# Attention and a two-layer network in one kernel: the words ahead of chunk 2 in another order

## The chip, the cores and the metric

The kernel runs on one core of one Trainium2 chip. The metric is device time in microseconds, and lower is better. A core has five engines with a queue each: TensorE (PE in the profile, its weight loads PEld), VectorE (DVE), ScalarE (ACT), GpSimd (POOL) and SyncE (SP). They run beside each other and wait for each other on semaphores. Loads and stores are issued by an engine's queue and carried out by 16 DMA engines.

## The reference

```python
# q, k, v: (8, 8, 576, 64); f: (8, 8, 576)
scores = (q @ k.T) / sqrt(64)
cum = cumsum(log(clip(f, 1e-4, 1)), -1)
scores = where(causal, -1e9, scores + cum[:, None] - cum[None, :])
attn = softmax(scores)                   # denominator + 1e-9
x = (attn @ v).transpose(0, 2, 1, 3).reshape(4608, 512)
h = x @ w_in                             # 512 -> 2048
out = gelu_tanh(h) @ w_out               # 2048 -> 512
```

## The kernel before

**Tiling.** The 64 pairs of batch and head are taken four at a time: 16 quads, two for each batch (heads 0 to 3, heads 4 to 7). A quad has its own buffers for q, k, the exponentials `pt` and the weighted values `vw`, two of each in turn, so quads 0, 2, 4 share one set and quads 1, 3, 5 the other. The result of attention goes transposed to `xT`. The network runs over 9 chunks of 512 tokens: a first layer on `xT`, gelu to `gT`, a second layer on `gT`. A batch has 576 tokens, so chunk 0 needs batch 0 alone (quads 0 and 1), and chunk 1 needs batches 0 and 1 (quads 0 to 3).

**What one quad does.** q and k are loaded in bf16 and brought into place by DVE (line 214, `transpose_words`). The scores come in rounds, transposed (keys by queries), by matmuls of 32 rows (line 283); ACT takes their exponential into `pt` (line 291); the causal part of the diagonal blocks is set to zero by POOL (line 297, `mask`) or multiplied by a triangle on DVE (line 327, `mask_by_product`). The factors of the forget gate, `wT`, weigh the values: `vw` (line 231). Products of 32 columns give the denominators (`denominators`, line 372 and after, two transposes and a reciprocal on DVE) and the output (`attn_out`, line 385, a product on DVE that writes `xT`). For quads 0 and 1 these are cut in two parts, queries 0 to 255 and 256 to 575 (line 339, tile `po_m`); later quads go in one piece (line 353, `po`).

**An order written out by hand.** Nothing is scheduled: each engine's queue holds its instructions in the order in which the words of a few tables are run. The table `FRONT` holds all that comes before chunk 2; `SECOND`, `STEADY`, `FLUSH` and `LAST` hold the rest. A word's numbers are the arguments of its operation. The words that matter here:

| word | what it does | engine |
|---|---|---|
| `LP.t`, `LC.b.t`, `LV.b.half` | load values: batch 0 tile t; batch b tile t; half of a batch's heads | issued by POOL, POOL, SP |
| `LQ.i`, `LK.i` | load q, k of quad i | issued by POOL |
| `WI.c`, `WO.c` | load an eighth of `w_in`, a quarter of `w_out` | issued by POOL |
| `TQ.i`, `TK.i` | bring q, k of quad i into place (`qT`, `kT`) | DVE |
| `SC`, `CT`, `CE.n` | running sums, their transposes, the factors `wT` | DVE, PE, ACT |
| `B.n.cols`, `BK.i.n` | n matmuls on zeros, of no use but to keep PE running; `BK` waits for `kT` and has 512 columns | PE |
| `S.i.r`, `H.i.r.g` | score round r of quad i: all heads; heads 2g and 2g+1 | PE, ACT |
| `M.i.r`, `m.i.r` | the masks of that round | POOL; DVE |
| `W.n`, `vw.i`, `VW.i`, `CL.i`, `cl.i` | factors in bf16; weighted values; a copy of their first block | DVE; DVE; POOL; DVE; ACT |
| `D.i.part`, `V.i.x.part`, `v.i.x` | denominators; half x of the output | PE, DVE |
| `j.half.g.n`, `J.half.g` | first layer of chunk 0 for half of its tokens, group g of four feature blocks; `j` in the spare accumulator, n matmuls at a time | PE, ACT |
| `RJ`, `GJ` | copy the raw sums of a group aside (line 417); their gelu | DVE; ACT |
| `I.c.pr` | first layer of chunk c, feature blocks 2pr and 2pr+1 (line 401) | PE, ACT |
| `F.c.n`, `f.c.n` | n units of chunk c's second layer, full or as four products of 32 columns (lines 690, 617) | PE, DVE, SP |
| `UW.u.k`, `PW.u.k`, `U.k`, `G` | sums of weights or gelus that chunks 1 and on use | DVE, POOL, DVE, DVE |
| `X`, `tr`, `UT` | load the exponential's table; the triangles | ACT, ACT, POOL |

**Buffers.** Scores and `J` groups take turns in two accumulators (tag `s`); `po_m` and the second layer in two smaller ones (`m`); the fill, `j` groups and `po` in one (`po`). So a score half waits for the exponential of the half before the last, and `j.0.1` waits until `RJ.0.0` has copied `j.0.0` away. A `j` group first runs the two of its four inner blocks that come from quad 0, then the two from quad 1; a `J` group runs three blocks and then, for all four feature blocks, the last one, which is `V.1.1`.

Of the kernel before, what the change touches and what calls it, by code (L numbers as in the profile page):

```python
# [16 lines left out]
def kernel(  # L17
# [12 lines left out]
    B, H, S, D = q.shape  # L30
# [38 lines left out]
    ON_ACT = ()  # L69

    FRONT = """
        LP.1 LP.4 SC LP.0 WI.0 B.8.512 B.1.512 CT TK.0 CE.1 TQ.0 CE.0 B.2.512 LP.3 B.1.128 BK.0.2 B.1.512 WI.5 B.1.512 S.0.0 TK.1 M.0.0 B.1.128
        B.1.128 WI.1 WI.2 B.1.128 BK.0.1 B.3.512 H.0.2.1 B.1.128 BK.0.1 H.0.2.0 WI.3 H.0.1.0 W.0 LP.2 TQ.1 D.0.0 H.1.0.0 vw.0.0 B.1.128 B.2.512
        BK.1.1 H.1.0.1 M.1.0 H.0.1.1 B.1.512 M.0.1 vw.1.0 V.0.1.0 B.1.128 B.1.512 V.0.0.0 H.0.3.0 UT D.1.0 j.0.0.4 V.1.0.0 V.1.1.0 H.1.3.1 WI.4 WI.7
        H.0.3.1 WI.6 j.0.0.4 j.0.0.8 H.1.1.0 RJ.0.0 M.0.3 WO.0 H.1.1.1 vw.0.1 LC.1.1 D.0.1 j.0.1.8 H.1.3.0 M.1.1 WO.1 M.1.3 H.1.2.1 V.0.0.1 VW.1.1
        V.0.1.1 UW.2.1 W.1 LQ.2 H.1.2.0 J.0.2 LK.2 LK.3 WO.2 D.1.1 j.0.1.8 GJ.0.1 V.1.0.1 V.1.1.1 TK.2 J.0.3 tr WO.3 J.1.1 TQ.2 GJ.0.0 LQ.3 U.0
        J.1.3 J.1.2 J.1.0 F.0.1 f.0.3 LC.1.2 LC.1.0 f.0.2 S.2.0 TK.3 X f.0.2 PW.2.2 F.0.7 LC.1.3 F.0.1 S.2.2 f.0.2 F.0.1 TQ.3 f.0.2 LC.1.4 LQ.4 LK.5
        f.0.4 S.2.1 F.0.1 f.0.4 LV.2.1 F.0.1 LK.4 F.0.3 M.2.2 F.0.1 vw.2 m.2.1 F.0.2 CL.2 LV.2.0 S.3.0 f.0.1 M.2.0 f.0.2 D.2 f.0.3 S.3.1 TQ.4 f.0.1
        LQ.6 VW.3 f.0.4 M.3.0 f.0.1 V.2.0 TK.4 S.3.2 f.0.6 V.2.1 m.3.1 S.4.1 f.0.4 LQ.5 f.0.1 H.4.2.0 f.0.2 M.3.2 H.4.2.1 cl.3 D.3 VW.4 H.4.0.0
        M.4.2.3 H.4.0.1 V.3.1 LK.6 v.3.0 f.0.1 F.0.1 I.1.2 I.1.0 TQ.5 U.1 TK.5 TQ.6 vw.5 I.1.5 UW.2.4 I.1.1 LV.3.1 LV.3.0 I.1.3 TK.6 U.3 I.1.4 U.2  # L80
        m.4.2.2 I.1.6 I.1.7 LK.7 X F.1.1 CL.5 F.1.2 M.4.1 G.0 G.1.1.2 F.1.4 cl.4 F.1.9 S.5.0 F.1.12 UW.2.3 m.4.0 F.1.4 M.5.0 F.1.4 F.1.5 S.5.1 D.4
        F.1.5 LQ.8 F.1.2 F.1.4 S.5.2 V.4.0 f.1.1 M.5.1 M.5.2.2 M.5.2.3 LK.8 f.1.11 V.4.1 S.6.0 f.1.3 D.5 LQ.7@m.3.1 M.6.0 f.1.10 S.6.1 vw.6 f.1.1
        V.5.1 f.1.1 F.1.9 CL.6 M.6.1 F.1.2 S.6.2 m.6.2.3 f.1.1 V.5.0 f.1.4 F.1.2 m.6.2.2
    """

    SECOND = """
# [33 lines left out]
    def many(n, shape, dtype, name):  # L120
        return [singles.tile(shape, dtype, name=f"{name}{i}") for i in range(n)]
# [11 lines left out]
    vw = many(2, [128, NT + 1, 4, D], BF16, "vw")  # L133
# [760 lines left out]
```

## Time and profile before

| what | value |
|---|---|
| median of 3 runs | 321.2 us (320.77 to 322.05) |
| profiled execution | 320.93 us, its span 319.2 us |
| granted TensorE clock | 1.00 |
| DMA | 33.41 MB, mean 105 GB/s |

The page gives each engine's busy time and share of the span, and the chain of work that ended last, followed back from the last instruction. A row of the timeline gives the start in us from the span's start, the length from the first to the last of the merged instructions, the engine, the line, the operation, what it writes and reads, the shape and count, and in brackets the idle time of the engine before it with what ended it. In the stretches each engine's busy time stands with its number of instructions, then the granted clock, the DMA share and GB/s. The end of a matmul is modelled, so two groups of PE can overlap; the difference of two starts is safer than a length.

### The profile page before, as it was taken

To read this page: it belongs to the slowest core of one execution; us is meant where nothing else is said; L and a number is where in the kernel's file an instruction comes from. 1 tells how busy PE (TensorE), PEld (TensorE's weight loads), DVE (VectorE), ACT (ScalarE), POOL (GpSimd) and SP (SyncE) were. 2 spreads that over 40 slices of the span, in tenths; PEclk is the share of its full clock that TensorE was granted. 3 is DMA by queue.
4 is the path that set the end of the run, shared out by engine and by line. 5 is a ranking of instruction groups with operands and counts; after the bars stand their busy time and mean duration, and the time that the engine had idled before them with its cause. 6 is when DMAs were issued, how large, how long until landed. Compare 5 with 4: busy or idle time off the path is not lost.

```text
span 319.2 us, 11780 instructions
## 1 busy us (share of the span) xinstructions
PE 313.2 (98%) x5318; PEld 219.1 (69%) x5318; DVE 243.0 (76%) x369; ACT 212.6 (67%) x246; POOL 109.3 (34%) x148
## 2 busy tenths in 40 slices
PE   7999999999999999999999999999999999999996
PEld 2467734545676577776788878767776786688785
DVE  7777438598878889879877987599876866597674
ACT  3766885966766876877767866787596744836610
POOL 8799541920340416410851075305610140000000
PEclk9999999999999999999999999999999999999999
DMA  7999999985253901593139411961001111010203
GB/s 126 222 203 204 208 227 218 176 156 103 45 105 103 215 7 39 120 206 74 39 87 224 89 39 36 213 152 38 5 34 67 35 36 35 28 40 2 101 33 100
DMA packets 47490, 33.41 MB, mean 105 GB/s; under 512 B 29776, under 2 KB 42192, under 8 KB 47440
## 3 DMA queue, kind: packets, MB, share of 16 engines
q0 software_dynamic: 9632, 15.99, 28.8%
q1 hardware_dynamic: 37664, 16.60, 19.5%
q8 instruction: 41, 0.67, 0.9%
q10 hardware_dynamic: 144, 0.07, 0.1%
q14 instruction: 9, 0.07, 0.1%
HBM read 36.85 MB, written 9.44 MB: 145 GB/s over the span
## 4 chain that ended last, share of the span: by engine, by line
PE 94%; DMA 3%; POOL 1%; DVE 1%; issue 0%; DVEq 0%; POOLq 0%
PE ps_w L617 31%; PE ps_h L401 20%; PE ps_q L537 10%; PE po L353 9%; PE ps_s L283 9%; PE pso L690 5%; PE ps_h L437 5%; PE ps_u L485 4%; DMA v_nat<-in_v_dram 3%; PE po_m L339 1%; PE ps_p L617 1%; POOL v_nat L184 0%; PE ps_o L353 0%; DVE usum L417 0%; POOL q_c L207 0%
## 5 line engine op out<-in xcount | busy, mean ns | idle before, releaser
L291 ACT ACTIVATE pt<-ps_s 128x1024 bf16<-128x1024 f32 (+2 forms) x100 | 94.1, 991 | 38.2 <-PE ps_s L283 36.6
L297 POOL TENSOR_SCALAR_AFFINE_SELECT pt<-pt 128x512 bf16<-128x512 bf16 (+3 forms) x73 | 45.9, 638 | 95.4 <-ACT pt L291 72.4
L401 PE MATMUL ps_h<-xT,w_in_sb 128*128 128x512 bf16 (+1 forms) x320 | 66.9, 358 | 0.0
L401 PEld LDWEIGHTS <-w_in_sb 128*128 128x128 bf16 x320 | 31.2, 98 | 26.1 <-issue 0.2
L617 PEld LDWEIGHTS <-gT 128*32 128x32 bf16 (+1 forms) x1171 | 44.0, 97 | 5.9 <-issue 2.4
L409 ACT ACTIVATE gT<-ps_h 128x1024 bf16<-128x1024 f32 x34 | 34.6, 1017 | 20.3 <-PE ps_h L401 20.1
L617 PE MATMUL ps_w<-w_out_sb,gT 128*32 128x256 bf16 (+1 forms) x996 | 42.5, 273 | 0.0
L617 PEld LDWEIGHTS <-gsum 128*32 128x32 bf16 (+1 forms) x903 | 35.3, 97 | 3.7 <-issue 1.3
L283 PE MATMUL ps_s<-qT,kT 32*128 32x64 bf16 (+5 forms) x896 | 35.4, 261 | 0.6 <-DVE qT L214 0.4
L553 DVE TENSOR_TENSOR usnap<-ps_q,usnap 128x1024 f32<-128x1024 f32 x15 | 17.9, 1220 | 17.3 <-PE ps_q L537 12.7
L617 PE MATMUL ps_w<-usum,gsum 128*32 128x256 bf16 (+1 forms) x749 | 30.1, 273 | 0.0
L283 PEld LDWEIGHTS <-kT 32*128 32x128 bf16 x896 | 16.3, 92 | 17.0 <-issue 10.2
L231 POOL TENSOR_TENSOR vw<-v_nat,wT 128x1280 bf16<-128x1280 f32 (+1 forms) x12 | 27.3, 2274 | 0.9 <-DMA v_nat<-in_v_dram 0.6
L634 DVE COPY snap<-ps_w 128x512 f32<-128x512 f32 x32 | 21.8, 680 | 6.7 <-PE ps_w L617 6.5
L214 DVE STREAM_TRANSPOSE kT<-k_c 128x576 f32<-128x576 f32 x16 | 19.4, 1243 | 6.8 <-DMA k_c<-in_k_dram 6.8
L385 DVE TENSOR_TENSOR xT<-po,rb 128x576 bf16<-128x576 f32 x26 | 19.5, 751 | 5.1 <-PE po L353 4.9
L548 ACT ACTIVATE gT<-usnap 128x1024 bf16<-128x1024 f32 x15 | 15.8, 1053 | 11.0 <-DVE usnap L553 10.7
L214 DVE STREAM_TRANSPOSE qT<-q_c 128x576 f32<-128x576 f32 x16 | 19.7, 1243 | 4.4 <-DMA q_c<-in_q_dram 4.4
L353 PE MATMUL po<-pt,vw 128*32 128x64 bf16 (+4 forms) x624 | 22.4, 278 | 0.0
L207 POOL DMA_DIRECT2D k_c<-in_k_dram x16 | 9.0, 565 | 35.7 <-DVE kT L214 23.5
L353 PEld LDWEIGHTS <-vw 128*32 128x32 bf16 x672 | 14.6, 97 | 9.3 <-issue 2.6
L537 PEld LDWEIGHTS <-w_in_sb 128*128 128x128 bf16 x160 | 15.6, 98 | 2.1
(134 smaller groups left out, 482.9 us busy)
## 6 DMA issues: line engine op xcount, KB each, us to landing
out_dram<-o_st SPq DMA_DIRECT2D x35, 256.0 KB, 2.2
k_c<-in_k_dram POOLq DMA_DIRECT2D x16, 288.0 KB, 5.7
q_c<-in_q_dram POOLq DMA_DIRECT2D x16, 288.0 KB, 5.7
v_nat<-in_v_dram SPq DMA_DIRECT2D x16, 256.0 KB, 4.9
v_nat<-in_v_dram SPq DMA_DIRECT2D x20, 128.0 KB, 5.4
v_nat<-in_v_dram POOLq DMA_DIRECT2D x8, 256.0 KB, 8.8
w_in_sb<-in_moe_w_in_dram POOLq DMA_DIRECT2D x8, 256.0 KB, 7.4
w_out_sb<-in_moe_w_out_dram POOLq DMA_DIRECT2D x4, 512.0 KB, 10.5
```

The costliest lines, as they stand in the source:

```text
L214: return nc.vector.transpose(out=dst.rearrange("p s c -> p (s c)").bitcast(FP32) .rearrange("p (t a) -> p a t", a=n), in_=src.rearrange("p ...
L231: return eng.tensor_mul(vw[i % 2][:, t0:t1], vb[:, t0:t1, h0:h0 + 4, :], wT[:, i, t0:t1, :].unsqueeze(3).to_broadcast([128, t1 - t0, 4, D]))
L283: nc.tensor.matmul(tiles[h // 2][:, h % 2, c0:c0 + nq], key_columns(i, key, h, c), qq[32 * h:32 * h + 32, q0:q0 + nq, c], start=(c == 0 an ...
L291: nc.scalar.activation(p[:, 2 * g:2 * g + 2, off:off + n], t[:, :, 0:n], AF.Exp, scale=scale)
L297: nc.gpsimd.affine_select(out=x, in_=x, compare_op=ALU.is_ge, fill=0.0, base=0, pattern=pattern, channel_multiplier=-1)
L353: nc.tensor.matmul(po[r0:r0 + w.shape[-1], 448 + q0:448 + q0 + nq], w, p[:, h, col:col + nq], start=(key in (0, "low")), stop=(key in ("lo ...
L385: nc.vector.tensor_mul(xT[:, 2 * u + x, r0 + s0:r0 + s1], po, rbs[i, part])
L401: nc.tensor.matmul(ph[:, j, n * cols:(n + 1) * cols], w_in_sb[:, dt, 128 * ft:128 * ft + 128], xT[:, dt, h0:h0 + cols], start=(dt == 0 and ...
L409: nc.scalar.activation(gelus(c, 2 * pr, 2), ph, AF.Gelu_apprx_tanh)
L537: nc.tensor.matmul(ps[:, k, HC * n:HC * n + HC], w[:, d, 128 * n:128 * n + 128], x[:, d, :], start=(first and n == 0 and d == 0), stop=(d ...
L617: nc.tensor.matmul(ps[c0:c0 + width, n, cols[0]:cols[1]], x[:, j, 128 * n + c0:128 * n + c0 + width], w[:, j, cols[0]:cols[1]], start=(fir ...
L634: copy(kept[name], ps)
```

## The change

One table, `FRONT`, is replaced. The multiset of its words stays almost the same: `UW.2.1` (DVE) becomes `PW.2.1` (POOL), `M.2.0` (POOL) becomes `m.2.0` (DVE), `CL.2` (DVE) becomes `cl.2` (ACT); there are 40 instead of 32 matmuls of fill (16,128 instead of 13,696 columns, all of the difference ahead of the first score round), and chunk 0's second layer has 21 full units and 43 of 32 columns instead of 19 and 45. The rest is order:

- values of batch 0 load as LP.0, LP.1, LP.3, LP.2, LP.4, with `WI.1` and `WI.0` after the first two; `LP.4` is issued after the masks M.1.0;
- `H.1.2.0` follows `H.0.3.0`, ahead of `D.1.0` (it stood after `V.0.1.1`); `V.1.1.0`, `H.0.3.1`, `V.1.0.0` and `H.1.3.1` follow, and all of `j.0.0` stands behind them in one piece (it stood in two, around these);
- `LQ.2` and `LK.2` are issued ahead of the four `WO`; the values of batch 1 (`LC.1.*`) after `LQ.3`;
- the second half of `j.0.1` goes ahead of `J.0.2`, and `J.0.3` between `V.1.0.1` and `V.1.1.1`; `TQ.2` stands on DVE between the last two products into `xT`;
- in chunk 0's second layer the units are spread differently between the score rounds of quads 2 to 4, and `V.2.0` comes after 42 units instead of 49.

```diff
     FRONT = """
-        LP.1 LP.4 SC LP.0 WI.0 B.8.512 B.1.512 CT TK.0 CE.1 TQ.0 CE.0 B.2.512 LP.3 B.1.128 BK.0.2 B.1.512 WI.5 B.1.512 S.0.0 TK.1 M.0.0 B.1.128
-        B.1.128 WI.1 WI.2 B.1.128 BK.0.1 B.3.512 H.0.2.1 B.1.128 BK.0.1 H.0.2.0 WI.3 H.0.1.0 W.0 LP.2 TQ.1 D.0.0 H.1.0.0 vw.0.0 B.1.128 B.2.512
-        BK.1.1 H.1.0.1 M.1.0 H.0.1.1 B.1.512 M.0.1 vw.1.0 V.0.1.0 B.1.128 B.1.512 V.0.0.0 H.0.3.0 UT D.1.0 j.0.0.4 V.1.0.0 V.1.1.0 H.1.3.1 WI.4 WI.7
-        H.0.3.1 WI.6 j.0.0.4 j.0.0.8 H.1.1.0 RJ.0.0 M.0.3 WO.0 H.1.1.1 vw.0.1 LC.1.1 D.0.1 j.0.1.8 H.1.3.0 M.1.1 WO.1 M.1.3 H.1.2.1 V.0.0.1 VW.1.1
-        V.0.1.1 UW.2.1 W.1 LQ.2 H.1.2.0 J.0.2 LK.2 LK.3 WO.2 D.1.1 j.0.1.8 GJ.0.1 V.1.0.1 V.1.1.1 TK.2 J.0.3 tr WO.3 J.1.1 TQ.2 GJ.0.0 LQ.3 U.0
-        J.1.3 J.1.2 J.1.0 F.0.1 f.0.3 LC.1.2 LC.1.0 f.0.2 S.2.0 TK.3 X f.0.2 PW.2.2 F.0.7 LC.1.3 F.0.1 S.2.2 f.0.2 F.0.1 TQ.3 f.0.2 LC.1.4 LQ.4 LK.5
-        f.0.4 S.2.1 F.0.1 f.0.4 LV.2.1 F.0.1 LK.4 F.0.3 M.2.2 F.0.1 vw.2 m.2.1 F.0.2 CL.2 LV.2.0 S.3.0 f.0.1 M.2.0 f.0.2 D.2 f.0.3 S.3.1 TQ.4 f.0.1
-        LQ.6 VW.3 f.0.4 M.3.0 f.0.1 V.2.0 TK.4 S.3.2 f.0.6 V.2.1 m.3.1 S.4.1 f.0.4 LQ.5 f.0.1 H.4.2.0 f.0.2 M.3.2 H.4.2.1 cl.3 D.3 VW.4 H.4.0.0
...
+        SC B.1.128 B.1.512 B.1.256 TK.0 B.8.512 B.1.512 B.1.128 LP.0 LP.1 CT CE.1 B.2.512 WI.1 WI.0 B.1.256 TQ.0 CE.0 B.1.128 LP.3 TK.1
+        BK.0.2 BK.0.1 B.1.512 B.1.512 BK.0.1 B.1.128 S.0.0 M.0.0 LP.2 B.1.128 BK.0.1 B.3.512 WI.2 H.0.2.1 WI.5 W.0 B.1.128 BK.0.1 TQ.1
+        B.1.128 B.1.128 WI.3 H.0.2.0 H.0.1.0 D.0.0 H.1.0.0 vw.0.0 B.2.512 BK.1.1 H.1.0.1 H.0.1.1 B.1.128 B.1.512 B.1.128 B.1.512 M.1.0
+        vw.1.0 V.0.1.0 V.0.0.0 H.0.3.0 LP.4 H.1.2.0 M.0.1 D.1.0 V.1.1.0 H.0.3.1 UT V.1.0.0 H.1.3.1 j.0.0.4 WI.4 j.0.0.4 M.0.3 j.0.0.8
+        H.1.1.0 H.1.1.1 RJ.0.0 WI.6 WI.7 LQ.2 LK.2 tr vw.0.1 D.0.1 j.0.1.8 WO.0 VW.1.1 H.1.2.1 H.1.3.0 V.0.0.1 V.0.1.1 j.0.1.8 M.1.1 W.1
+        GJ.0.0 M.1.3 J.0.2 D.1.1 V.1.0.1 GJ.0.1 TQ.2 J.0.3 V.1.1.1 J.1.2 WO.1 WO.2 J.1.1 J.1.0 LK.3 WO.3 J.1.3 PW.2.1 LQ.3 LC.1.0 PW.2.2
+        F.0.1 U.0 F.0.1 f.0.1 LC.1.1 f.0.2 LC.1.2 f.0.2 LC.1.4 LC.1.3 TK.2 TK.3 LQ.4 LK.4 S.2.0 F.0.1 X F.0.8 m.2.0 S.2.2 f.0.2 F.0.2 f.0.6
+        S.2.1 TQ.3 f.0.3 F.0.7 m.2.1 vw.2 LV.2.1 S.3.0 f.0.3 M.2.2 D.2 f.0.2 TQ.4 cl.2 LV.2.0 M.3.0 f.0.1 S.3.1 V.2.0 f.0.2 LQ.5 VW.3 f.0.3
+        LK.5 LV.3.1 f.0.1 S.3.2 LV.3.0 LQ.6 f.0.1 TK.4 m.3.1 f.0.1 M.3.2 V.2.1 f.0.5 S.4.1 LK.6 VW.4 f.0.6 H.4.2.0 f.0.1 H.4.2.1 TQ.5
...
     """
```

More of the change, by code (lines that the diff above doesn't have):

```diff
@@ L80 @@
[L80 to L83, printed above, removed]
+        SC B.1.128 B.1.512 B.1.256 TK.0 B.8.512 B.1.512 B.1.128 LP.0 LP.1 CT CE.1 B.2.512 WI.1 WI.0 B.1.256 TQ.0 CE.0 B.1.128 LP.3 TK.1
@@ L84 @@
+        M.4.2.3 cl.3 D.3 X H.4.0.0 H.4.0.1 V.3.1 v.3.0 f.0.1 vw.5 m.4.2.2 CL.5 UW.2.4 F.0.1 I.1.4 I.1.0 U.1 U.2 TK.5 LK.7 TQ.6 I.1.5 I.1.2
+        I.1.1 G.0 I.1.3 TK.6 U.3 I.1.6 I.1.7 G.1.1.2 F.1.3 M.4.1 F.1.5 cl.4 F.1.6 S.5.0 LK.8 F.1.14 UW.2.3 m.4.0 F.1.4 M.5.0 F.1.3 S.5.1 D.4
+        F.1.15 LQ.8 F.1.2 S.5.2 M.5.2.2 M.5.1 M.5.2.3 f.1.2 V.4.0 f.1.10 V.4.1 LQ.7@m.3.1 S.6.0 M.6.0 f.1.3 D.5 f.1.12 vw.6 S.6.1 V.5.1
+        F.1.8 CL.6 M.6.1 F.1.3 S.6.2 m.6.2.3 V.5.0 f.1.5 m.6.2.2 F.1.2
     """
```

## Prediction

> **What bounds the kernel now.** I read the page first, then the busy time in stretches of 8 us, then every engine in order of time from 0 to 68 us. The page says that TensorE is busy nearly all the time and that the chain that ended last lies on it:
>
> ```profile
> span 319.2 us, 11780 instructions
> PE 313.2 (98%) x5318; PEld 219.1 (69%) x5318; DVE 243.0 (76%) x369; ACT 212.6 (67%) x246; POOL 109.3 (34%) x148
> PE 94%; DMA 3%; POOL 1%; DVE 1%; issue 0%; DVEq 0%; POOLq 0%
> ...
> 8.00:16.00 8.00, 7.28 (x94) 3.25 (x96) 5.75 (x10) 6.21 (x8) 5.80 (x9) 1.00 1.12 222
> 16.00:24.00 8.00, 7.89 (x152) 5.09 (x156) 5.65 (x12) 5.16 (x8) 7.68 (x14) 1.00 1.18 203
> 24.00:32.00 8.00, 8.00 (x139) 6.11 (x124) 5.62 (x11) 5.18 (x7) 7.45 (x11) 1.00 1.18 204
> 32.00:40.00 8.00, 8.00 (x88) 6.20 (x90) 3.97 (x4) 6.55 (x10) 4.15 (x5) 1.00 1.18 208
> ```
>
> The columns after the length are the busy times of PE, PEld, DVE, ACT and POOL, the granted clock (1.00 all through) and the DMA share. PE shows idle time only up to 24 us (0.72 + 0.11 in two stretches); the DMA share stays above 1 until 40 us, so the loads queue one behind the other there. The change moves words but no product of chunk 2 or later, so it can win only what PE loses ahead of that: waits, idle-filling matmuls, and the pause between kinds of matmul. These rows show the losses, with the steps that the change touches:
>
> ```profile
> 7.39 1.26 DVE L214 STREAM_TRANSPOSE qT<-q_c 128x576 f32<-128x576 f32 x1 [0.19 <-DMA q_c<-in_q_dram]
> 8.71 0.52 PE L283 MATMUL ps_s<-qT,kT 32*128 32x256 bf16 x16 [0.42 <-DVE qT L214]
> ...
> 12.57 0.29 PEld L283 LDWEIGHTS <-kT 32*128 32x128 bf16 x8 [0.36 <-DVE qT L214]
> 14.52 1.29 DVE L231 TENSOR_TENSOR vw<-v_nat,wT 128x512 bf16<-128x512 f32 x2 [0.85 <-DMA v_nat<-in_v_dram]
> 15.26 0.12 PEld L339 LDWEIGHTS <-vw 128*32 128x32 bf16 x8 [0.44 <-DVE vw L231]
> 15.27 2.22 POOL L297 TENSOR_SCALAR_AFFINE_SELECT pt<-pt 128x512 bf16<-128x512 bf16 x3 [0.20 <-ACT pt L291]
> 15.27 0.35 PE L339 MATMUL po_m<-pt,vw 128*32 128x256 bf16 x8
> 15.55 0.45 PE L256 MATMUL idle_ps<-idle 128*128 128x128 bf16 x2
> 16.20 0.51 PE L283 MATMUL ps_s<-qT,kT 32*128 32x320 bf16 x8
> 16.65 0.53 PE L339 MATMUL po_m<-pt,w_bf 128*32 128x256 bf16 x8
> 17.11 0.61 PE L437 MATMUL ps_h<-xT,w_in_sb 128*128 128x256 bf16 x4
> 18.89 1.48 PE L437 MATMUL ps_h<-xT,w_in_sb 128*128 128x256 bf16 x12
> 20.30 0.65 PE L283 MATMUL ps_s<-qT,kT 32*128 32x320 bf16 x16
> 20.41 1.22 DVE L417 COPY usum<-ps_h 128x1024 f32<-128x1024 f32 x1 [1.15 <-PE ps_h L437]
> 21.68 1.03 PE L437 MATMUL ps_h<-xT,w_in_sb 128*128 128x256 bf16 x8
> 21.93 0.96 DVE L231 TENSOR_TENSOR vw<-v_nat,wT 128x768 bf16<-128x768 f32 x1 [0.30 <-DMA v_nat<-in_v_dram]
> 23.35 1.22 PE L339 MATMUL po_m<-pt,vw 128*32 128x320 bf16 x40
> 24.50 0.46 PE L283 MATMUL ps_s<-qT,kT 32*128 32x320 bf16 x4
> 24.89 1.92 PE L437 MATMUL ps_h<-xT,w_in_sb 128*128 128x256 bf16 x16
> 29.51 8.91 PE L437 MATMUL ps_h<-xT,w_in_sb 128*128 128x256 bf16 x80
> 38.25 1.57 PE L690 MATMUL pso<-w_out_sb,gT 128*128 128x512 bf16 x21
> 50.46 1.02 PE L353 MATMUL po<-pt,w_bf 128*32 128x512 bf16 x24
> 53.94 0.85 PE L353 MATMUL po<-pt,vw 128*32 128x512 bf16 x24
> 54.72 0.69 PE L283 MATMUL ps_s<-qT,kT 32*128 32x320 bf16 x16
> ```
>
> First number: start; second: length. **Two prices** come out of them. The 80 full matmuls of 256 columns run from 29.51 until the next group at 38.25: 8.74 / 20,480 = 0.427 ns a column. The 24 products at 53.94 run four abreast over 64+512+448+320+192+64 = 1600 columns, 0.68 us at that rate, but the next group starts 0.78 us later: a change of kind (32-row scores, 32-column products, full matmuls) costs 0.10 us.
>
> **The change part by part.** *Ahead of the first score round (8.71).* The fill ahead of the column sums grows from 4608 to 5632 columns, from there to S.0.0 from 3200 to 4608. Both end in time: PE waited 0.42 us for qT, 1408 more columns are 0.60 us at full rate, and 0.20 of that I place in the wait for kT before the fill that reads it, so S.0.0 stays at about 8.7, since q is still the second load issued and qT ends at 7.39+1.26 = 8.65. Cost 0, at worst 0.1. After S.0.0 both versions have 5888 columns of fill.
>
> *First values (15.3 to 17.1).* V.0.1.0 and V.0.0.0 lose the fill between them (15.55 to the start of the second product, about 0.37); 0.33 of fill goes ahead of the first, where PE waited 0.44 for vw anyway. So H.0.3.0 starts near 15.85 instead of 16.20. LP.0 and LP.1 now load ahead of LP.4, so vw can only come sooner. Then H.1.2.0 stands there too. The following D.1.0 needs the first two of the three masks at 15.27 (0.74 each, so done at 16.75), and the mask cannot start sooner than its exponential; PE has 0.7 us of score work to fill 15.85 to 16.6. The gain in place is used up by H.1.2.0: D.1.0 stays within 0.2 of 16.65, and H.1.2.0 is done for nothing. In the version before it cost 24.50 to 24.89, 0.39 with its two changes of kind.
>
> *First-layer groups behind the scores (17.1 to 24.5).* j.0.0 now runs as 4+4+8 in one piece after V.1.0.0 and H.1.3.1: same matmuls, same four changes of kind, end within 0.2 of 20.2. Behind it the copy on DVE (1.22, it waited 1.15 for ps_h) still frees the accumulator ahead of j.0.1 at 21.68: 0 to 0.2 sooner. That is lost again at V.0.0.1 (23.35), which needs vw.0.1, which waited for a v load at 21.93; that load is now LP.4 instead of LP.2, but the ten transfers up to it are the same ten. So at 24.5 the lead is H.1.2.0 alone, 0.39. From there to the output product the rest has one more change than before without that pair (J.0.3 between V.1.0.1 and V.1.1.1): +0.1, and -0.05 for half of what j.0.1 may keep. The output product starts at about 37.9 instead of 38.25: **-0.35**.
>
> *Work that changes engine.* UW.2.1 leaves DVE for POOL as PW.2.1; mask 2.0 goes from POOL to DVE, copy_low 2 from DVE to ACT.
>
> ```profile
> 25.04 2.06 DVE L467 TENSOR_TENSOR wsum<-w_in_sb 128x512 bf16<-128x512 bf16 x1
> 25.33 1.48 POOL L231 TENSOR_TENSOR vw<-v_nat,wT 128x768 bf16<-128x768 f32 x1
> 26.75 0.68 POOL L207 DMA_DIRECT2D q_c<-in_q_dram  x1
> 27.43 1.08 POOL L207 DMA_DIRECT2D k_c<-in_k_dram  x2
> 34.39 1.18 POOL L469 TENSOR_TENSOR wsum<-wsum,w_in_sb 128x512 bf16<-128x512 bf16 x1
> 36.03 1.26 DVE L214 STREAM_TRANSPOSE kT<-k_c 128x576 f32<-128x576 f32 x1 [5.91 <-DMA k_c<-in_k_dram]
> 43.15 0.53 POOL L207 DMA_DIRECT2D k_c<-in_k_dram  x1 [1.74 <-DMA w_out_sb<-in_moe_w_out_dram]
> 48.99 1.49 DVE L231 TENSOR_TENSOR vw<-v_nat,wT 128x1280 bf16<-128x1280 f32 x1 [0.18 <-DMA v_nat<-in_v_dram]
> 62.02 0.40 ACT L236 COPY vw<-vw 64x256 bf16<-64x256 bf16 x1
> ```
>
> The add was hidden on DVE (PE ran full matmuls beside it) and is worth 0 there. On POOL its price is between 1.18 (its sister) and 2.06; I take 1.2. Behind it in POOL's queue stand LQ.3 and the v loads of batch 1, which are long in the DMA queue, so 0. [...]
>
> *Loads.* LQ.2 and LK.2 pass w_out parts 0 to 3, and part 1 to 3 now wait on POOL behind VW.1.1 (1.48) and the last masks, to about 26.7. Part 0 is used at 37.9, so 0. LQ.2's landing matters, because its transpose TQ.2 stands on DVE between the last two products that write xT; that is the first rival.
>
> *Output product of chunk 0 with quads 2 to 4 (38 to 65).* In the programs' own order I count the changes of kind: from the first score round to the output product 29 become 26 (what is worth anything of these is in the 0.35), from there to chunk 1's output product 27 become 25, afterwards 15 and 55 in both. **-0.2**. D.2's 24 products took 1.02 at 50.46 where the same shapes took 0.85 at 53.94, a wait of 0.17 for masks that two more DVE products may end sooner: 0 to -0.17; I take **-0.05**. copy_low's 0.40 on ACT lies ahead of V.2.0, beside output matmuls: 0, with the rest of its price in rival 2.
>
> **Sum:** -0.35 - 0.2 - 0.05 = -0.6 us. The profiled execution took 320.93 (span 319.2 and 1.7 around it), so 320.3 by it; the median 321.2 is 0.27 above, which gives 320.6 for a median.
>
> **Rivals.** *1, slower: TQ.2 waits for q.* LQ.2 is issued at about 21.5 (M.0.3 follows the exponential of H.0.3.1, whose group stands just ahead of 18.1 now, and ends near 20.1; two issues of 0.7 each follow, by the row at 26.75). TQ.2 (1.25) is queued on DVE ahead of xT of V.1.1.1, which J.1.2 needs for its last four matmuls, near 32.4. DVE needs 1.25 + 0.5, so q may land up to 30.65. For it: the queue is full there, and k of the same quad took 27.43 to 36.03, 8.6 us, in the version before. Against: 21.5 + 8.6 = 30.1, and the issue comes ahead of the large w_out parts. From 30.65 on every us late costs a us; if q landed as late as it must have before (the next load, k, at 36.03, less about 1.3, so 34.7) it costs 4.1: 320.6 + 4.1 = 324.7; midway 322.7. The decider is whether w_in's parts 6 and 7 hold it.
>
> *2, nothing left.* The lead is given back between 49 and 55 us: vw.2 waited for batch 1's v (48.99), which now stand behind both POOL adds, and V.2.0 comes after 42 instead of 49 units of chunk 0's output product. V.2.0 was at 53.94 and vw.2 ended at 50.48, 3.5 of slack; seven units of 512 columns less are 1.5, so 2.0 are left, less the 0.4 of copy_low on ACT. v later by 2.2 eats the lead: 320.6 + 0.6 = 321.2. Against: 43.15 shows that POOL's issue itself waits for an old landing, so the queue is full and the same set of transfers ends at the same time.
>
> *3, all waits go.* The visible waits after 8.71 (0.36 for qT at 12.57, 0.44 for vw, some 0.2 ahead of 21.68 for the copy, 0.17 at 50.46) and five changes of kind (0.5) are 1.7 together: 321.2 - 1.7 = 319.5. For it: POOL's long stretch (7.68 of 8 from 16 to 24) loses nothing but the masks come sooner. Against: three of those waits hang on loads in the same order of bytes.
>
> **How the numbers follow.** Forecast (320.0 to 321.0) 0.48; rival 1 0.22; rival 2 0.18; rival 3 0.12. Half a per cent is 1.6 us, about what a measurement of this kernel can tell from no change. Forecast and rival 2 lie within it: 0.66. Rival 1 counts as slower from 322.8 on; with the same wait at other late loads I give it all of its 0.22. Rival 3 just passes 319.6: 0.12. The range takes in rival 3, with 0.3 for the runs' own spread (320.77 to 322.05 about 321.2), and two thirds of rival 1: 319.2 to 323.4.
>
> **What would show it.** Right: PE's first output matmul of chunk 0 near 37.9; ps_s groups of quads 0 and 1 done by 23.3; no score group between V.0.1.1 and J.0.2; DVE's qT of quad 2 ended ahead of 31. Wrong: a PE wait in front of the last matmuls of J.1.2 (rival 1), a vw row after 51 or a wait at V.2.0 (rival 2), S.0.0 later than 8.8 (fill too long), or a first output matmul ahead of 37.2 (rival 3).

## The result: slower by one per cent, outside the range

The changed kernel took 324.69 us (median of 6 runs, 323.03 to 327.17), the kernel before 321.06 (6 runs, 320.77 to 322.36): a ratio of 1.0104, 95% interval 1.006 to 1.0149. The forecast was 320.6. Of the profiled execution (323.65 us) first three lines of the page, then the stretches that answer to those shown of before, with the same columns:

```profile
span 321.9 us, 11770 instructions
PE 312.4 (97%) x5302; PEld 220.4 (68%) x5320; DVE 245.4 (76%) x368; ACT 212.8 (66%) x247; POOL 110.4 (34%) x147
PE 88%; ACT 3%; DMA 3%; POOL 2%; DVE 1%; issue 1%; DVEq 0%
```

```profile
16.00:24.00 8.00, 7.37 (x128) 4.56 (x124) 3.69 (x9) 6.07 (x10) 7.27 (x14) 1.00 1.09 172
24.00:32.00 8.00, 5.95 (x106) 4.80 (x107) 6.36 (x11) 5.12 (x6) 8.00 (x11) 1.00 1.16 195
32.00:40.00 8.00, 8.00 (x89) 6.87 (x87) 4.47 (x5) 4.10 (x4) 5.33 (x6) 1.00 1.22 207
```

PE was busy all of 24 to 32 before, now for 5.95 of 8 us; the DMA share ahead of it (16 to 24) fell from 1.18 to 1.09. The timeline of the changed kernel names the place:

```profile
16.30 0.72 POOL L185 DMA_DIRECT2D v_nat<-in_v_dram  x1
23.26 0.46 PE L340 MATMUL po_m<-pt,vw 128*32 128x320 bf16 x8
23.71 1.47 POOL L232 TENSOR_TENSOR vw<-v_nat,wT 128x768 bf16<-128x768 f32 x1 [0.64 <-DMA v_nat<-in_v_dram]
23.76 2.24 DVE L232 TENSOR_TENSOR vw<-v_nat,wT 128x768 bf16<-128x768 f32 x1 [2.27 <-DMA v_nat<-in_v_dram]
26.05 1.13 PE L340 MATMUL po_m<-pt,vw 128*32 128x320 bf16 x32 [2.33 <-DVE vw L232]
30.99 1.92 PE L438 MATMUL ps_h<-xT,w_in_sb 128*128 128x256 bf16 x16
32.42 1.25 DVE L215 STREAM_TRANSPOSE qT<-q_c 128x576 f32<-128x576 f32 x1
40.47 0.92 PE L691 MATMUL pso<-w_out_sb,gT 128*128 128x512 bf16 x3
```

This is V.0.0.1. Its first eight matmuls run on the tiles that are there; the others wait for vw.0.1, which waits for LP.4, issued at 16.30. Before, vw.0.1 began at 21.93 and took 0.96; now it begins at 23.76 and takes 2.24, beside POOL's VW.1.1, which had waited for the same load.

LP.4 is the tenth of the loads that POOL issues from 4 us on, as LP.2 was before, and the ten are the same ten. In the profiles of both kernels the ten landed in the order in which they were issued (from 12.58 to 21.84 before, from 11.79 to 23.64 now). LP.4, issued at 16.30, landed at 23.64, only 0.38 behind the ninth, which had been issued at 14.41: so it was not its own issue that held it, but all that stood in front of it was late. POOL's rows of the kernel before, where the tenth landed at 21.84:

```profile
8.14 0.70 POOL L196 DMA_DIRECT2D w_in_sb<-in_moe_w_in_dram  x1
10.85 1.22 POOL L297 TENSOR_SCALAR_AFFINE_SELECT pt<-pt 128x512 bf16<-128x512 bf16 x2 [2.00 <-ACT pt L291]
12.03 2.14 POOL L196 DMA_DIRECT2D w_in_sb<-in_moe_w_in_dram  x3
14.17 0.90 POOL L184 DMA_DIRECT2D v_nat<-in_v_dram  x1
```

and of the changed kernel:

```profile
7.34 0.90 POOL L185 DMA_DIRECT2D v_nat<-in_v_dram  x1
10.91 1.23 POOL L298 TENSOR_SCALAR_AFFINE_SELECT pt<-pt 128x512 bf16<-128x512 bf16 x2 [2.68 <-ACT pt L292]
12.10 0.90 POOL L185 DMA_DIRECT2D v_nat<-in_v_dram  x1
13.00 2.11 POOL L197 DMA_DIRECT2D w_in_sb<-in_moe_w_in_dram  x3
```

The masks at 10.9 wait for an exponential, and POOL issues nothing until they are done. Before, six loads were issued ahead of them; now five are, since LP.4 no longer stands there. The first five, LP.4's place now taken by a load of twice its size, landed by 16.54 (16.08 before). The sixth came 1.86 behind the fifth and the eighth 2.35 behind the seventh, where such a step took 1.20 and 1.28 before. Why is not shown; that one load fewer was issued ahead of the masks is a guess that the step of the sixth speaks for.

Two things, then: a load that lands 1.8 us later, and an operation that is 1.28 us longer. A third is not in this profile. In all 12 runs made of the changed kernel (6 here, 6 in E5), the two with a mean granted clock of 1.0 took 323.03 and 323.65; those at 0.994 or 0.995 took 324.62 to 326.13, those at 0.99 or 0.989 took 326.44 to 329.02. Of 71 runs of the kernel before, ten stood at 0.995, none lower, and those ten took 321.37 to 321.89.

**One table for all profiles.** The distances are worked out from the traces: the start of the first matmul of each stage, less the start of the one before. "Out 0" is chunk 0's output product, "v.3.0" the first half of quad 3's output, "out 1" chunk 1's second layer, "in 2" the first product by the sums (ps_u) in chunk 2's first layer, "last" the last matmul of ps_p.

| kernel | S.0.0 at | to out 0 | to v.3.0 | to out 1 | to in 2 | to last |
|---|---|---|---|---|---|---|
| before | 8.71 | 29.55 | 25.27 | 15.11 | 22.55 | 214.86 |
| changed | 8.77 | 31.70 | 25.41 | 15.10 | 22.90 | 214.86 |
| E1 LP.4 early | 9.08 | 29.35 | 25.44 | 15.11 | 22.90 | 214.87 |
| E2 VW.1.1 later | 8.76 | 29.70 | 25.43 | 15.11 | 22.90 | 214.87 |
| E3 both | 8.77 | 29.02 | 25.43 | 15.10 | 22.91 | 214.87 |
| E4 before, LP.4 late | 8.62 | 30.91 | 25.15 | 15.12 | 22.55 | 214.87 |
| E5 changed, again | 10.89 | 34.95 | 25.41 | 15.11 | 22.89 | 214.87 |
| E6 pause filled | 8.82 | 31.29 | 25.43 | 15.10 | 22.90 | 214.87 |
| E7 table load moved | 9.26 | 29.01 | 25.36 | 15.11 | 23.13 | 214.87 |
| E8 and units | 8.73 | 29.02 | 25.56 | 15.11 | 22.55 | 214.87 |
| E9 before, scores early | 9.62 | 28.95 | 25.16 | 15.12 | 22.55 | 214.85 |
| E10 before, side by side | 9.87 | 29.84 | 26.88 | 15.12 | 23.21 | 214.85 |

The changed kernel loses 2.15 ahead of out 0, 0.14 ahead of v.3.0 and 0.35 between out 1 and in 2; nothing behind that.

### The profile page after: what moved, and what is told of

Its sections match the earlier page's. It is cut to its first block, busy times and chain, and to the rows that moved or that the text cites. A ratio compares the mean times of both kernels' runs of the same rounds, so it can differ in the third digit from the quotient of the medians.

```text
span 321.9 us, 11770 instructions
## 1 busy us (share of the span) xinstructions
PE 312.4 (97%) x5302; PEld 220.4 (68%) x5320; DVE 245.4 (76%) x368; ACT 212.8 (66%) x247; POOL 110.4 (34%) x147
## 4 chain that ended last, share of the span: by engine, by line
PE 88%; ACT 3%; DMA 3%; POOL 2%; DVE 1%; issue 1%; DVEq 0%
PE ps_w L618 29%; PE ps_h L402 19%; PE ps_q L538 10%; PE po L354 9%; PE ps_s L284 7%; PE pso L691 4%; PE ps_u L486 4%; PE ps_h L438 4%; ACT pt L292 2%; DMA v_nat<-in_v_dram 2%; PE po_m L340 1%; DMA f_all<-in_f_dram 1%; DVE vw L232 1%; POOL w_in_sb L197 1%; POOL pt L298 1%
## 5 line engine op out<-in xcount | busy, mean ns | idle before, releaser
L402 PE MATMUL ps_h<-xT,w_in_sb 128*128 128x512 bf16 (+1 forms) x308 | 65.6, 357 | 0.9 <-issue 0.3
L284 PE MATMUL ps_s<-qT,kT 32*128 32x64 bf16 (+5 forms) x896 | 36.1, 261 | 0.6 <-ACT pt L292 0.2
## 6 DMA issues: line engine op xcount, KB each, us to landing
w_out_sb<-in_moe_w_out_dram POOLq DMA_DIRECT2D x4, 512.0 KB, 10.9
```

Source lines behind the costliest of these rows:

```text
L284: nc.tensor.matmul(tiles[h // 2][:, h % 2, c0:c0 + nq], key_columns(i, key, h, c), qq[32 * h:32 * h + 32, q0:q0 + nq, c], start=(c == 0 an ...
L402: nc.tensor.matmul(ph[:, j, n * cols:(n + 1) * cols], w_in_sb[:, dt, 128 * ft:128 * ft + 128], xT[:, dt, h0:h0 + cols], start=(dt == 0 and ...
```

## The experiments

Theory after the result: LP.4 is issued too late, and its landing starts two operations at once, of which DVE's then takes 2.24 us instead of 0.96. Rivals: only the order of the load counts; only the neighbour counts; or the words that were moved for their own sake (scores, first-layer groups) cost the time. The kernel before, run beside each, took 321.41 us (29 runs, E1 to E4), 321.37 (22 runs, E5 to E8) and 321.29 (20 runs, E9 and E10).

### E1: the load alone

```diff
-CE.0 B.1.128 LP.3 TK.1          ... H.0.3.0 LP.4 H.1.2.0
+CE.0 B.1.128 LP.3 LP.4 TK.1     ... H.0.3.0 H.1.2.0
```

> The changed kernel with LP.4 issued right behind LP.3 (as the version before issued it among the first loads) instead of behind the masks M.1.0. Theory (TensorE stands 2.5 us at V.0.0.1 because vw.0.1 waits for LP.4's landing at 23.6 us): vw.0.1 runs near 21.6 to 22.0, the stall goes, the time falls by about 2.5 us and, if the lower granted clock of some runs comes from that stall, by more: 320.5 to 322.2. Rival (the DMA queue as a whole is late and LP.4 only shows it): the wait comes back at the next load in line, at the second half of j.0.1 or at J.0.2, and the time stays above 323.5.

Measured: 321.11 us (320.84 to 321.65, 12 runs), ratio 0.9996 (0.9987 to 1.0005), granted clock 1.0 in every run. From its timeline:

```profile
22.05 1.67 DVE L232 TENSOR_TENSOR vw<-v_nat,wT 128x768 bf16<-128x768 f32 x1
23.51 1.53 POOL L232 TENSOR_TENSOR vw<-v_nat,wT 128x768 bf16<-128x768 f32 x1
```

vw.0.1 waits for no load any more and is done before its products are due. One word is the whole loss. The tenth load, now a part of w_in, still landed at 22.50, 0.66 later than before, but vw.0.1 does not need it: the last of its values are the seventh load (LP.2), which landed at 18.85. The operation is still longer than 0.96, although POOL's VW.1.1 starts 1.46 later and runs beside it for 0.21 only; what lengthened it is not shown, and it hides here.

### E2: the neighbour alone

```diff
-WO.0 VW.1.1 H.1.2.1 ... GJ.0.0 M.1.3 J.0.2
+WO.0 H.1.2.1 ... GJ.0.0 M.1.3 VW.1.1 J.0.2
```

> The changed kernel with VW.1.1 on GpSimd behind the masks M.1.1 and M.1.3, LP.4 left late. Theory (the DVE product vw.0.1 took 2.24 instead of 0.96 us because GpSimd's VW.1.1 began at the same landing and held it off): vw.0.1 takes about 0.96 us, the stall shrinks from 2.5 to about 1.2 us, time near 323.4. Rival (2.24 is no effect of GpSimd's product): vw.0.1 stays near 2.2 us, time unchanged at 324.7.

Measured: 322.45 us (321.63 to 324.23, 12 runs), ratio 1.0036 (1.0022 to 1.005). From its timeline:

```profile
23.02 0.96 DVE L232 TENSOR_TENSOR vw<-v_nat,wT 128x768 bf16<-128x768 f32 x1 [1.14 <-DMA v_nat<-in_v_dram]
26.29 1.50 POOL L232 TENSOR_TENSOR vw<-v_nat,wT 128x768 bf16<-128x768 f32 x1
```

Without POOL's operation beside it vw.0.1 takes 0.96, as before the change; it still waits for the load. So both parts count: the late load alone costs about 1.0 (322.45 - 321.41). The two together cost 3.6 in the first runs, with the clock in it (E5 and E6).

### E3: both

The two edits together.

> Both edits. Theory: with LP.4 early DVE's vw.0.1 (near 22) and VW.1.1 (near 24) no longer meet, so the second edit adds nothing: within 0.3 us of the run with LP.4 early alone, 320.5 to 322.2. [...]

Measured: 321.07 us (320.81 to 321.31, 12 runs), ratio 0.9996 (0.9987 to 1.0006): no faster than E1's 321.11, so with LP.4 early the neighbour costs nothing that shows. Timeline of PE and ACT:

```profile
37.79 1.79 PE L691 MATMUL pso<-w_out_sb,gT 128*128 128x512 bf16 x21
79.99 1.28 ACT L292 ACT_TABLE_LOAD   x1
81.28 1.94 ACT L292 ACTIVATE pt<-ps_s 128x1024 bf16<-128x1024 f32 x2
82.97 0.93 PE L284 MATMUL ps_s<-qT,kT 32*128 32x64 bf16 x16
```

Here chunk 0's output product stands where the prediction had put it (37.9), 0.46 ahead of 38.25. The lead is gone at the end. The group at 82.97 is S.5.1, and in the trace 0.28 of its length is a wait: its second half needs the accumulator that the second of the two exponentials at 81.28 frees (81.28 + 1.94 = 83.22).

### E4: the late load in the kernel before

```diff
-LP.1 LP.4 SC LP.0 ... H.1.0.1 M.1.0 H.0.1.1
+LP.1 SC LP.0 ... H.1.0.1 M.1.0 LP.4 H.0.1.1
```

> The version before with LP.4 alone moved behind the masks M.1.0, as in the changed kernel. If the late issue by itself delays the landing (some 6 to 7 us from issue to landing): LP.4 lands at 23 to 24 us instead of by 21.8, V.0.0.1 stalls 1 to 2 us, time 322.0 to 323.0. If only the order of the bytes in a full queue counts, as the prediction had it: landing by 21.9, time 321.1 plus or minus 0.3.

Measured: 322.82 us (321.8 to 323.14, 6 runs), ratio 1.0044 (1.0027 to 1.0062). From its timeline:

```profile
16.34 0.70 POOL L184 DMA_DIRECT2D v_nat<-in_v_dram  x1
23.70 0.96 DVE L231 TENSOR_TENSOR vw<-v_nat,wT 128x768 bf16<-128x768 f32 x1 [2.58 <-DMA w_in_sb<-in_moe_w_in_dram]
24.72 1.13 PE L339 MATMUL po_m<-pt,vw 128*32 128x320 bf16 x32 [1.33 <-DVE vw L231]
```

The same load, issued at the same time, lets vw.0.1 start at the same time in the kernel before, with all its other words in place (23.70 against 23.76; the bracket names another DMA that ended near it as the releaser, but the moved load is the only edit). The ten transfers up to it are those of before in both versions, so "the same ten, hence the same landing" is refuted. LP.4 landed at 23.62. Here too the loads in front of it were late: LP.2, issued at 14.09 (14.17 before), landed at 22.82 instead of 21.84, although LP.4 no longer stood ahead of it. VW.1.1 stands apart there, and the operation takes 0.96.

### E5 and E6: does the pause cost clock?

E5 is the changed kernel once more, E6 the same with ten matmuls on zeros where PE stands:

```diff
 po = psM.tile([128, 512], FP32, name="po_m", tag="m")
+if i == 0 and part == 1:
+    seen.append(1)
+    if len(seen) == 2:
+        for _ in range(10):
+            nc.tensor.matmul(po, idle[:, 0:128], idle, start=True, stop=True)
```

> The changed kernel itself once more, as the measure for the next run. Theory (the pause of 2.5 us ahead of the products of vw.0.1 also costs granted clock later): most runs again show a granted clock below 0.999, and the median is 324 to 325, 1.010 times the kernel before. Rival (the lower clock of the first six runs was chance and is not tied to the kernel): the clock is 1.0 as in the kernel before, and the median is 323.4, ratio 1.006.

> The changed kernel, with ten matmuls on zeros of 512 columns (2.1 us) at the place of the pause, into the accumulator that the products behind it overwrite. They take nothing away from the wait for vw.0.1: the output product of chunk 0 still starts near 40.4. Theory (the pause costs clock): every run at 0.999 or above, median 323.2 to 323.8. Rival (the clock has nothing to do with the pause): as many runs below 0.999 as in the run of the changed kernel beside it, same median as there.

Measured: E5 326.29 us (325.0 to 329.02, 6 runs), ratio 1.0146 (1.013 to 1.0162), clock 0.989 to 0.995 in all six; E6 324.05 (323.29 to 325.32, 6 runs), ratio 1.0096 (1.0077 to 1.0115), clock 0.999 or 1.0 in all six. E5's profile, the slowest of its runs, in stretches and in rows:

```profile
24.00:32.00 8.00, 4.74 (x66) 2.76 (x64) 6.67 (x7) 5.25 (x8) 7.99 (x11) 0.72 1.08 169
32.00:40.00 8.00, 8.00 (x106) 6.06 (x105) 5.47 (x9) 2.96 (x3) 5.20 (x7) 0.85 1.24 209
```

```profile
25.15 3.88 DVE L232 TENSOR_TENSOR vw<-v_nat,wT 128x768 bf16<-128x768 f32 x1 [1.55 <-DMA v_nat<-in_v_dram]
25.20 1.49 POOL L232 TENSOR_TENSOR vw<-v_nat,wT 128x768 bf16<-128x768 f32 x1
26.63 1.59 POOL L298 TENSOR_SCALAR_AFFINE_SELECT pt<-pt 128x512 bf16<-128x512 bf16 x3
29.09 1.69 PE L340 MATMUL po_m<-pt,vw 128*32 128x320 bf16 x32 [3.26 <-DVE vw L232]
30.71 3.60 PE L438 MATMUL ps_h<-xT,w_in_sb 128*128 128x256 bf16 x16
```

and E6 at the same place:

```profile
23.29 2.24 DVE L232 TENSOR_TENSOR vw<-v_nat,wT 128x768 bf16<-128x768 f32 x1 [1.73 <-DMA v_nat<-in_v_dram]
23.56 2.10 PE L343 MATMUL po_m<-idle 128*128 128x512 bf16 x9 [0.16 <-issue]
25.60 1.22 PE L347 MATMUL po_m<-pt,vw 128*32 128x320 bf16 x40
```

In E5 vw.0.1 took 3.88, 2.9 more than 0.96, and ended at 29.03, behind POOL's operation and the three masks after it (28.22); PE stood 3.3, and the granted clock fell to 0.72 and 0.85. The sixteen matmuls that took 1.92 in the first profile of the changed kernel took 3.60 here: about half the rate. With the pause filled, the delay of the products stays (out 0 at 31.29 instead of 31.70 behind S.0.0) and the clock does not fall, in any run; 2.2 us of the median go (both medians lie above what was expected, by 1.3 and 0.25). So the changed kernel pays twice: about 2.7 with the pause filled (324.05 - 321.37; 2.63 in its first profile's distances, of which 2.15 lie ahead of out 0), and for the clock after it 0.9 in the first six runs (324.69 - 321.06 - 2.7) and 2.2 in the next six. The two figures for the clock are differences of medians, partly from different series, and so estimates. Among the first six, the runs below a clock of 1.0 (median 324.88) lie 1.5 above the two at 1.0 (mean 323.34).

E5's profile has more than the pause in it. Its S.0.0 came 2.12 later than in the first profile (10.89 against 8.77), which the last section takes up. Of the 3.25 more from there to out 0, 0.91 is a later vw.0.1 (it ended 18.14 behind S.0.0, against 17.23), and 2.34 lies behind that, in the stretches with the lower clock.

How long a pause has to be for that is not shown. An idle time of 2.33 us ahead of the products (the row at 26.05) left the clock at 1.00 in one execution, 3.26 (the row at 29.09) did not in another.

### E7 and E8: where E3's lead goes

The first table load moved (X from ahead of H.4.0.0, where the table is in place, to behind I.1.7), then also the units of chunk 1 as before:

```diff
 E7, on top of E3:
-D.3 X H.4.0.0 ... I.1.7 G.1.1.2
+D.3 H.4.0.0 ... I.1.7 X G.1.1.2
 E8, on top of E7:
-G.1.1.2 F.1.3 M.4.1 F.1.5 cl.4 F.1.6 S.5.0 ... (to the end of the table)
+F.1.1 F.1.2 M.4.1 G.1.1.2 F.1.4 cl.4 F.1.9 S.5.0 ... (as in the kernel before)
```

> The changed kernel with the two repairs of e3 (LP.4 early, VW.1.1 behind M.1.3), and the word X moved from ahead of H.4.0.0, where the exponential's table is in place already and ACT only spends 0.20 us, to behind I.1.7, as in the kernel before. Theory (e3's lead of 0.46 us is lost at H.4.0.0 and at S.5.0, because ACT is late there): the lead at chunk 1's output product is 0.4 or more, the wait of 0.28 at 82.97 goes, the end is 0.2 to 0.4 ahead of e3: 320.7 to 320.9, ratio about 0.998. Rival (the lead is lost to the place of S.5.0 among the units): the wait stays, and the time is e3's, 321.1.

> As e7, and all words from G.1.1.2 to the end of the first table as in the kernel before (16 units of chunk 1's output product ahead of S.5.0 instead of 14, and so on). Theory (ACT is late by the table load): no more than 0.1 better than e7. Rival (the place of S.5.0 decides): this one is 0.3 ahead of e7, near 320.8. If both say right the kernel stands near 320.7, ratio 0.9975 to 0.998, and is the best of all.

Measured: E7 321.3 us (320.99 to 323.21, 12 runs), ratio 1.0006 (0.9994 to 1.0018); E8 320.62 (320.44 to 321.15, 11 runs), ratio 0.9976 (0.9966 to 0.9987). ACT in E7:

```profile
79.98 1.28 ACT L246 ACT_TABLE_LOAD   x1
81.28 0.20 ACT L246 ACTIVATE spare<-shift 1x1 f32<-1x1 f32 x1
81.50 0.40 ACT L237 COPY vw<-vw 64x256 bf16<-64x256 bf16 x1
81.93 1.94 ACT L292 ACTIVATE pt<-ps_s 128x1024 bf16<-128x1024 f32 x2
```

E3's load stands at 79.99 and E7's at 79.98, but E7's S.0.0 came 0.49 later. Counted from out 1 (78.32 and 78.74) the load starts 1.24 behind it in E7 instead of 1.67, so the word does bring it forward by 0.43. The gain is used up: the copy cl.4 (0.40), which ran ahead of the load in E3, now runs behind it, and the explicit word's own exponential adds 0.20. The exponentials start 3.19 behind out 1 instead of 2.96, and the distance from out 1 to in 2 grows from 22.91 to 23.13. My theory fell. With 16 units ahead of S.5.0 instead of 14 and 25 from there to S.5.1 instead of 21, and the rest as before, it is 22.55 again, and the wait in S.5.1 is gone, though the exponentials start as late as in E7 (3.19 behind out 1): the rival holds. E8 is the only version here whose interval lies clear of the kernel before on the faster side, by 0.24%.

### E9: one word alone

```diff
-V.0.0.0 H.0.3.0 UT D.1.0 ... LQ.2 H.1.2.0 J.0.2
+V.0.0.0 H.0.3.0 H.1.2.0 UT D.1.0 ... LQ.2 J.0.2
```

> The kernel before, with one word moved: H.1.2.0 behind H.0.3.0, as in the change, instead of ahead of J.0.2. Theory (the prediction's term of 0.39: the pair of score groups rides free behind V.0.0.0, where D.1.0 waits for a mask anyway, and takes its two changes of kind with it): the output product of chunk 0 starts 0.3 to 0.5 ahead of 38.25, and the end is 0.2 to 0.4 sooner, ratio 0.999. Rival (D.1.0 does not wait that long, so the group only changes its place): the output product starts 0.1 to 0.2 sooner at most, the ratio is 1.000.

Measured: 321.05 us (320.16 to 325.46, 12 runs), ratio 0.9995 (0.9978 to 1.0011): by the times, nothing is shown (the one run at 325.46, which the ratio leaves out, had a granted clock of 0.989, in an order without LP.4's late issue; what lowered it there is not shown). The distances of the profile show more, since this execution's S.0.0 came 0.91 later than before's. From its timeline:

```profile
9.62 0.53 PE L283 MATMUL ps_s<-qT,kT 32*128 32x256 bf16 x16
...
16.73 0.80 PE L283 MATMUL ps_s<-qT,kT 32*128 32x320 bf16 x12
17.46 0.35 PE L339 MATMUL po_m<-pt,w_bf 128*32 128x256 bf16 x8
...
38.57 1.57 PE L690 MATMUL pso<-w_out_sb,gT 128*128 128x512 bf16 x21
```

D.1.0, at 17.46, follows the pair of groups at 16.73 without a wait, and out 0 stands 28.95 behind S.0.0 instead of 29.55. But not all of this 0.60 is the word's: 0.38 is there ahead of its new place, where H.0.3.0 stands 7.11 behind S.0.0 (16.73 - 9.62) instead of 7.49 (16.20 - 8.71), because less is waited for q and for the values behind an S.0.0 that comes later. That leaves 0.22 for the word, between the rival's 0.1 to 0.2 and the theory's 0.3 to 0.5.

### E10: the two operations started together, no load late

```diff
-RJ.0.0 M.0.3 WO.0 H.1.1.1 vw.0.1 ... V.0.0.1 VW.1.1
+RJ.0.0 M.0.3 VW.1.1 WO.0 H.1.1.1 vw.0.1 ... V.0.0.1
```

> The kernel before, with VW.1.1 moved ahead of WO.0 on POOL, so that both weighted values, vw.0.1 on DVE and VW.1.1 on POOL, wait for the same load and start beside each other near 21.9; no load is later than before ahead of that. Theory (two operations of that kind, started together, hold DVE's for longer): vw.0.1 takes about 2.2 instead of 0.96 and ends near 24.2, so V.0.0.1 stands 0.8 to 1.0 later than 23.35, and the time is 0.6 to 1.0 above before: 322.0 to 322.4. Rival (the 2.24 came from the late load alone): vw.0.1 takes about 1.0, and the time is that of before.

Measured: 323.13 us (321.77 to 325.25, 9 runs), ratio 1.0053 (1.0027 to 1.0078). The direction was forecast, the reason was not. From its timeline:

```profile
22.29 0.96 DVE L231 TENSOR_TENSOR vw<-v_nat,wT 128x768 bf16<-128x768 f32 x1
22.34 2.24 POOL L231 TENSOR_TENSOR vw<-v_nat,wT 128x768 bf16<-128x768 f32 x1 [0.35 <-DVE usum L417]
...
28.33 0.57 PE L339 MATMUL po_m<-pt,w_bf 128*1 128x320 bf16 x12 [0.46 <-POOL pt L297]
52.07 1.49 DVE L231 TENSOR_TENSOR vw<-v_nat,wT 128x1280 bf16<-128x1280 f32 x1 [1.56 <-DMA v_nat<-in_v_dram]
53.95 0.61 PE L353 MATMUL po<-pt,w_bf 128*1 128x448 bf16 x16 [1.38 <-DVE pt L327]
```

The two start 0.05 apart again, and this time POOL's takes 2.24 and DVE's 0.96. PE does not wait for vw.0.1; it waits for the masks behind VW.1.1 (0.46), and 25 us later for a mask on DVE behind vw.2, because the loads of batch 1 were issued later on POOL (one of them at 34.09, at 31.07 before). So which of the two takes longer beside the other isn't fixed: DVE's in the changed kernel (2.24, POOL's 1.47), POOL's here (2.24, DVE's 0.96). And the issues behind a longer POOL operation go out later: LC.1.1's at 25.34 here, at 22.03 before.

The order of the starts doesn't settle which: in the changed kernel POOL's started first (23.71 against 23.76) and DVE's took longer, in E10 DVE's started first (22.29 against 22.34) and POOL's took longer, but in E5 DVE's started first as well (25.15 against 25.20) and took 3.88 all the same.

## Why the prediction was wrong

**The step that failed** is in the part on the first-layer groups: "that load is now LP.4 instead of LP.2, but the ten transfers up to it are the same ten". It took a landing to follow from the bytes ahead of it alone, because the loads "queue one behind the other"; its evidence was a mean DMA share of 1.18 over 8 us. The tenth load landed at 21.84 before and at 23.64 now, and vw.0.1, which needs it, began at 21.93 and 23.76. E4 shows that LP.4 in the tenth place is enough to delay vw.0.1 so, and E1 that an early LP.4 takes the whole loss away. The same ten transfers ended at quite different times:

| kernel | ahead of M.0.0 | tenth issued | tenth landed |
|---|---|---|---|
| before | 6 loads | 14.17 (LP.2) | 21.84 |
| E9, E10 | 6 | 15.10, 15.44 (LP.2) | 23.04, 22.19 |
| E1, E3 | 6 | 14.70, 14.40 (WI.3) | 22.50, 23.33 |
| E7, E8 | 6 | 14.89, 14.36 (WI.3) | 22.31, 23.03 |
| changed, E5 | 5 | 16.30, 18.42 (LP.4) | 23.64, 25.03 |
| E2, E6 | 5 | 16.67, 16.34 (LP.4) | 22.89, 23.17 |
| E4 | 5 | 16.34 (LP.4) | 23.62 |

The fastest landing of all is that of the kernel before, and the prediction counted on it with a slack of 0.46. Part of the spread is the start (S.0.0 came 0.9 to 2.1 later in E5, E9 and E10). What else makes the tenth land early or late stays open: with LP.4 in its place it landed at 22.89 or later, with others at 21.84 to 23.33. Where the last values stand sixth and seventh (E1, E3, E7, E8), vw.0.1 does not feel it.

**The row that was read for the wrong pair.** The prediction's third fence has a DVE operation of 2.06 beside a POOL operation of 1.48 (25.04 and 25.33); in E10, where POOL's had ended at 24.58, the same DVE operation, at 25.71, takes 0.58. The prediction used the 2.06 only as a bound for the price of PW.2.1, which took 1.20, as taken. It did not ask which other pair the change brings together. LP.4's landing starts two at once, and E2 takes that part out.

**The clock** was in no step: the prediction took 1.00 all through for granted. E6 shows that the pause costs clock as well. By the medians this is about a quarter to a half of the loss (an estimate): 0.9 of 3.6 in the first runs, 2.2 of 4.9 in the second.

**The terms of the sum.** Ahead of S.0.0: 0 was right (8.77 against 8.71). To the output product: -0.35 was forecast; with LP.4 early and VW.1.1 out of the way E3 has 29.02 against 29.55, -0.53. Of that 0.13 is there by V.0.0.1 (14.51 behind S.0.0 against 14.64), and 0.39 is the score group that no longer stands behind it. The word that E9 moves alone is worth 0.22. In the changed kernel the pause of 2.51 and 0.17 more in the products behind it stand against that: 2.51 + 0.17 - 0.53 = 2.15, as the table has it. From there to v.3.0: -0.2 and -0.05 were forecast for two changes of kind less and D.2's wait; +0.14 was measured. In E3 the gain is there at first: up to H.4.0 the order is 0.31 ahead of before's (23.09 behind out 0 against 23.40). It is lost at H.4.0, which takes 1.39 instead of 1.01, in part by a wait of 0.25 for an exponential where before's is 0.09, with the units differently around it; V.3.1 behind it adds 0.08. From out 1 to in 2: forecast 0, since the changes of kind are 15 in both; measured +0.35, by the places of S.5.0 and S.5.1 among the units (E8), which the change moves in chunk 1 too: 14 instead of 16 ahead of S.5.0.

**The rivals.** Rival 1 gave 324.7, and the median came out there, by another mechanism: TQ.2's row at 32.42 has no wait in its bracket, and PE stands nowhere ahead of J.1.2 (8.00 busy from 32 to 40). That is no hit. At rival 2's place (vw.2, V.2.0, between out 0 and v.3.0) 0.14 was lost, not 0.6. Rival 3's waits did go in part (the values at 15.21 and D.2 at 52.27 have none), but the pause ahead of V.0.0.1 is larger than all of them.

## What to carry to other kernels

A mean DMA share above 1 (1.18 before, 1.09 now, from 16 to 24 us) did not fix when a load lands: the same ten transfers, in other orders, ended 1.8 us apart and more. For each load that is moved, write down its place in the order of issue before and after, and check the operation that needs the load against the slack in the profile (here 0.46 us, 22.89 to 23.35). When a load gates operations on two engines, keep one of them away from the landing (vw.0.1 took 0.96 us so in E2, 2.24 in the changed kernel). And the pause on TensorE cost more behind it through the clock, 0.9 us in the first six runs and 2.2 in the next (estimates); filling it with idle matmuls gave 2.2 us back here without touching its cause.

## What the runs showed of the hardware that was not expected

In some executions the fill matmuls ahead of the first scores run at half the rate for longer, and the clock column doesn't show it: in E5 three fill matmuls of 512 columns ran from 8.44 to 9.71, 0.42 each, where they took 0.21 in the first profile of the changed kernel, and S.0.0 stood at 10.89 instead of 8.77, with the column at 1.00 from 8 to 16. E9's fill ran at 0.42 as well (S.0.0 at 9.62). A longer fill there, as the change has, would cost twice its length in such an execution (an estimate from these two rates: the 1408 more columns 1.2 us instead of 0.6), and the starts of S.0.0 in the table are not properties of the order alone.

A small load did not pass the loads ahead of it: LP.4, the last 64 keys of a batch and so half of the others' size, needed 7.3 us from its issue at 16.30 to its landing, with a DMA share of 1.09 around it; it landed 0.38 behind the load issued ahead of it.
